# Moving the gMLP's first half ahead of the state-space part, through HBM, with a second buffer for the CT loop

## The chip, the cores and the metric

One Trainium2 chip, one of its cores. The metric is the time of one execution on the device in microseconds (us); lower is better. Each kernel was run several times, beside runs of the kernel before on the same chip. Engines are named as in the profile: PE is TensorE, PEld its weight loads, DVE is VectorE, ACT is ScalarE, POOL is GpSimd, SP is SyncE. A name such as SPq or ACTq is the queue in which that engine issues transfers. PSUM is the memory, in banks, into which PE writes its sums; in this kernel ACT and DVE copy them out (such as Hst<-ps_mm). The granted clock is the share of PE's full clock that the profile shows for a stretch. A line of a timeline reads: start and length in us, engine, line of the kernel, operation, output<-input, shapes, count, and in brackets how long the engine had idled before and what ended that.

## The reference, cut to what matters

The output is the input plus two branches of its layer norm: a state-space convolution (A) and a gated MLP that mixes along the sequence (B). S is 2048, D is 512, N is 128, half of the MLP's width is 688.

```python
x = A_u
xn = _layernorm(x, axis=-1)
return x + _A_ref(xn, A_A_re, ..., A_Dskip) + _B_ref(xn, B_w_in, B_w_sp, B_b_sp, B_w_out)

# A: y = conv(xn, K) + xn * Dskip, where K[d, l] = Re sum_n C * exp(dt * A * l) * dt * B
# B:
z = _gelu(jnp.einsum('bsd,df->bsf', x, w_in))
z1 = z[..., :Fh].copy()
z2 = _layernorm(z[..., Fh:], axis=-1)
g = jnp.einsum('ts,bsf->btf', w_sp, z2) + b_sp[None, :, None]
return jnp.einsum('bsf,fd->bsd', z1 * g, w_out)
```

## The kernel before

The kernel turns A into blocks of 128 steps. The exponential is interpolated at 8 nodes (table E), its transpose ET is regrouped by many small copies into CT, matmuls with CT give the block states Hst, a recurrence over the blocks follows on VectorE, and matmuls of Hst with CWb give G. Inside a block, kappa and Lk do the convolution. B is the GELU part, called z (halves z1 and z2), then the mix over the sequence (the "spatial" groups), then the output product. The order of emission is: layer norm, E, CT loop, w_in and z2, recurrence, G, z1, final loop over eight chunks of 256 rows.

The parts that matter:

```python
# CT loop: 8 turns, ONE buffer, 32 row copies a turn
engs = [nc.scalar, nc.gpsimd]
for dq in range(NDQ):
    CT = sp.tile([P, DQ, 2, N], dt.bfloat16, name="CT", tag="CT")
    for g in range(ND):
        for k in range(KB):
            row = 32 * g + k
            engs[(g * KB + k) % len(engs)].dma_start(
                CT[row:row + 1, :, :, :].rearrange("o d c n -> o (d c n)"),
                ET2[dq * DQ:(dq + 1) * DQ, g, :, k, :])
    ...   # 128 matmuls into 4 PSUM banks, then 4 copies on ACT and 4 on DVE into Hst

# gelu: ACT copy, ACT square, DVE product, ACT sigmoid, DVE product
# z2, row by row: after two gelus
nc.scalar.activation(out=rstd[:], in_=mv[:, 1:2], func=ACT.Sqrt, bias=epsT[:])

# G: four times 256 matmuls and 4 copies (here one round's copies), with the order (dl s) turned into (s dl)
for h in range(4):
    d0 = b * P + h * 32
    nc.any.tensor_copy(out=G[:, :, d0:d0 + 32].rearrange("k s dl -> k dl s"),
                       in_=psg[32 * h:32 * h + KB, :].rearrange("k (dl s) -> k dl s", dl=32))
```

Of the kernel before, what the change touches and what calls it, by code (L numbers as in the profile page):

```python
# [11 lines left out]
dt = mybir.dt  # L12
ACT = mybir.ActivationFunctionType
ALU = mybir.AluOpType
# [3 lines left out]
P = 128  # L18
KB = 8
# [16 lines left out]
def kernel(  # L36
# [18 lines left out]
    nc = tc.nc  # L55
# [4 lines left out]
    S, D = x_flat.shape  # L60
    N = A_A_re.shape[1]
# [49 lines left out]
    G = keep.tile([KB, NT, D], dt.bfloat16, name="G")  # L111
    kapB = keep.tile([P, KB, D], dt.bfloat16, name="kapB")
    Lk = keep.tile([P, KB, P], dt.bfloat16, name="Lk")
# [47 lines left out]
    with tc.tile_pool(name="prep", bufs=1) as pp:  # L161
# [5 lines left out]
        for i, (nm, ap) in enumerate((("are", A_A_re), ("aim", A_A_im), ("bre", A_B_re),  # L167
                                      ("bim", A_B_im), ("cre", A_C_re), ("cim", A_C_im))):
            t = pp.tile([P, D], dt.bfloat16, name="prm_" + nm)
            (nc.sync if i % 2 == 0 else nc.scalar).dma_start_transpose(t[:], ap)  # L170
            prm[nm] = t
# [68 lines left out]
    engs = [nc.scalar, nc.gpsimd]  # L240
    for dq in range(NDQ):
        CT = sp.tile([P, DQ, 2, N], dt.bfloat16, name="CT", tag="CT")
# [44 lines left out]
    onesM = sp.tile([P, P], dt.bfloat16, name="onesM")  # L287
    nc.vector.memset(onesM[:], 1.0)
    cw_flat = CWb[:, 0, :, :].rearrange("p k d -> p (k d)")
    kap_flat = kapB[:].rearrange("p k d -> p (k d)")  # L290
    for i in range(KB * D // TCH):
        psk = psum.tile([P, TCH], dt.float32, name="ps_mm", tag="ps_mm", bufs=PSB)
        nc.tensor.matmul(psk[:], lhsT=onesM[:], rhs=cw_flat[:, i * TCH:(i + 1) * TCH],
                         start=True, stop=True)
        nc.any.tensor_copy(out=kap_flat[:, i * TCH:(i + 1) * TCH], in_=psk[:])

    u_i = sp.tile([P, P], dt.int32, name="u_i")
    nc.gpsimd.iota(u_i[:], pattern=[[1, P]], base=-64, channel_multiplier=-1)
    s_f = sp.tile([P, P], dt.float32, name="s_f")
    nc.vector.tensor_copy(out=s_f[:], in_=u_i[:])  # L300
    nc.vector.tensor_scalar(out=s_f[:], in0=s_f[:], scalar1=1.0 / 64.0, scalar2=None,
                            op0=ALU.mult)
    lk_f = sp.tile([P, P], dt.float32, name="lk_f")
    for k in range(KB):
        c = coefs[k]
        nc.vector.memset(lk_f[:], float(c[0]))
        for sidx in range(1, KB):
            nc.vector.tensor_tensor(out=lk_f[:], in0=lk_f[:], in1=s_f[:], op=ALU.mult)  # L308
            nc.vector.tensor_scalar(out=lk_f[:], in0=lk_f[:], scalar1=float(c[sidx]),
                                    scalar2=None, op0=ALU.add)  # L310
        nc.gpsimd.affine_select(out=lk_f[:], in_=lk_f[:], pattern=[[1, P]],
                                compare_op=ALU.is_ge, fill=0.0, base=0,
                                channel_multiplier=-1)
        nc.scalar.copy(out=Lk[:, k, :], in_=lk_f[:])

# [3 lines left out]
    if dbg in ("ssm", "intra", "inter"):  # L319
        gp = ctx.enter_context(tc.tile_pool(name="gmlp_dbg", bufs=1))  # L320
        for q in range(1, NT - 1):
# [54 lines left out]
    gmlp = ctx.enter_context(ExitStack())  # L376
    gpk = gmlp.enter_context(tc.tile_pool(name="gmlpk", bufs=1))
# [4 lines left out]
    z1T = gpk.tile([P, NF, S], dt.bfloat16, name="z1T")  # L382
    z2n = gpk.tile([P, NT, Fh], dt.bfloat16, name="z2n")
    gpz = ExitStack()
    gp = gpz.enter_context(tc.tile_pool(name="gmlpz", bufs=1))
    xnT = gp.tile([P, ND, S], dt.bfloat16, name="xnT")
    for dtl in range(ND):
        for g4 in range(NT // 4):
            pst = psum.tile([P, TCH], dt.bfloat16, name="ps_tr", tag="ps_tr")
            for i in range(4):  # L390
                q = g4 * 4 + i
                nc.tensor.transpose(out=pst[:, i * P:(i + 1) * P],
                                    in_=xnTok[:, q, dtl * P:(dtl + 1) * P],
                                    identity=ident[:])
            nc.any.tensor_copy(out=xnT[:, dtl, g4 * TCH:(g4 + 1) * TCH], in_=pst[:])
    w_in_sb = gp.tile([P, ND, F], dt.bfloat16, name="w_in_sb")
    nc.sync.dma_start(w_in_sb[:], B_w_in.rearrange("(t p) f -> p t f", p=P))

    SQC3 = math.sqrt(0.044715)
    C1 = 2.0 * math.sqrt(2.0 / math.pi)  # L400

    def gelu(ps_ap, dst_ap, rows, cols):
        zb = gp.tile([P, TCH], dt.bfloat16, name="g_zb", tag="g_zb", bufs=2)
        qd = gp.tile([P, TCH], dt.bfloat16, name="g_qd", tag="g_qd", bufs=2)
        sv = gp.tile([P, TCH], dt.bfloat16, name="g_sv", tag="g_sv", bufs=2)
        nc.scalar.activation(out=zb[0:rows, 0:cols], in_=ps_ap, func=ACT.Copy)  # L406
        nc.scalar.activation(out=qd[0:rows, 0:cols], in_=ps_ap, func=ACT.Square, scale=SQC3)  # L407
        nc.vector.scalar_tensor_tensor(out=sv[0:rows, 0:cols], in0=qd[0:rows, 0:cols],  # L408
                                       scalar=1.0, in1=zb[0:rows, 0:cols],
                                       op0=ALU.add, op1=ALU.mult)  # L410
        nc.scalar.activation(out=sv[0:rows, 0:cols], in_=sv[0:rows, 0:cols],  # L411
                             func=ACT.Sigmoid, scale=C1)
        nc.vector.tensor_tensor(out=dst_ap, in0=sv[0:rows, 0:cols], in1=zb[0:rows, 0:cols],  # L413
                                op=ALU.mult)

    f2_chunks = []
    c0 = 0
    while c0 < Fh:
        c1 = min(Fh, c0 + TCH)
        f2_chunks.append((c0, c1))  # L420
        c0 = c1
    for q in range(NT):
        z2g = gp.tile([P, Fh], dt.bfloat16, name="z2g", tag="z2g", bufs=2)
        for (c0, c1) in f2_chunks:
            ps = psum.tile([P, TCH], dt.float32, name="ps_mm", tag="ps_mm", bufs=PSB)
            for dtl in range(ND):
                nc.tensor.matmul(ps[:, 0:c1 - c0],  # L427
                                 lhsT=xnT[:, dtl, q * P:(q + 1) * P],
                                 rhs=w_in_sb[:, dtl, Fh + c0:Fh + c1],
                                 start=(dtl == 0), stop=(dtl == ND - 1))  # L430
            gelu(ps[:, 0:c1 - c0], z2g[:, c0:c1], P, c1 - c0)
        nsub = 2
        sub = Fh // nsub
        assert Fh % nsub == 0 and sub <= nc.vector.BN_STATS_FMAX
        stats = gp.tile([P, nsub, nc.vector.BN_STATS_DIM], dt.float32, name="z2_stats", bufs=3)
        for si in range(nsub):
            nc.vector.bn_stats(out=stats[:, si, :], in_=z2g[:, si * sub:(si + 1) * sub])  # L437
        mv = gp.tile([P, nc.vector.BN_AGGR_DIM], dt.float32, name="z2_aggr", bufs=3)
        nc.vector.bn_aggr(out=mv[:], in_=stats[:])
        rstd = gp.tile([P, 1], dt.float32, name="z2_rstd", bufs=3)  # L440
        nc.scalar.activation(out=rstd[:], in_=mv[:, 1:2], func=ACT.Sqrt, bias=epsT[:])
        nc.vector.reciprocal(out=rstd[:], in_=rstd[:])
        nc.vector.tensor_scalar(out=z2n[:, q, :], in0=z2g[:], scalar1=mv[:, 0:1],
                                scalar2=rstd[:, 0:1], op0=ALU.subtract, op1=ALU.mult)

# [30 lines left out]
    for ft in range(NF):  # L476
        fs = fsizes[ft]
        for tchk in range(NTC):
            ps = psum.tile([P, TCH], dt.float32, name="ps_mm", tag="ps_mm", bufs=PSB)
            for dtl in range(ND):  # L480
                nc.tensor.matmul(ps[0:fs, :],  # L481
                                 lhsT=w_in_sb[:, dtl, ft * P:ft * P + fs],
                                 rhs=xnT[:, dtl, tchk * TCH:(tchk + 1) * TCH],
                                 start=(dtl == 0), stop=(dtl == ND - 1))
            gelu(ps[0:fs, :], z1T[0:fs, ft, tchk * TCH:(tchk + 1) * TCH], fs, TCH)
    gpz.close()

    gt = gmlp.enter_context(tc.tile_pool(name="gt", bufs=1))
# [7 lines left out]
    for tchk in range(NTG):  # L496
# [3 lines left out]
        tsl = slice(tchk * TCG, (tchk + 1) * TCG)  # L500
        for ft in range(NF):
            fs = fsizes[ft]
            ps2 = psum.tile([P, TCH], dt.float32, name="ps_mm", tag="ps_mm", bufs=PSB)
            for st in range(NT):
                nc.tensor.matmul(ps2[0:fs, 0:TCG], lhsT=z2n[:, st, ft * P:ft * P + fs],  # L505
                                 rhs=wsT[:, st, :], start=(st == 0), stop=False)
# [71 lines left out]
```

## Time and profile before

The median is 600.23 us of the first 5 runs and 600.92 us of the 16 runs beside which the changed kernel was timed; the profiled run spans 598.5 us. The table gives the stages, read off the trace as first start and last end of the named instructions. These six moments are the ruler.

| us from the span's start | before |
|---|---|
| z on ACT | 266.8 to 426.5 |
| first CT copy issued | 121.2 |
| last Hst copy ended (CT loop done) | 255.5 |
| recurrence on DVE | 258.5 to 327.6 |
| G copies | 346.5 to 388.0 |
| first spatial matmul, then end of span | 435.9, 598.5 |

Busy time over the whole span is PE 49%, DVE 64%, ACT 41%, POOL 18%: no engine is full, so the stages must be read one by one. From the first spatial group on, PE is full and nothing else matters; before that, the question is always which engine the next stage waits for.

### The profile page before, as it was taken

The page shows a single profiled execution, that of the slowest core. Times are in us where ns is not written, and L with a number is a line of the kernel's source. Part 1 is how long each engine was busy: PE and PEld are TensorE (multiplying, and loading weights), DVE is VectorE, ACT ScalarE, POOL GpSimd, SP SyncE. Part 2 cuts the span into 40 slices and gives each one's busy share as a digit, 9 for nine tenths or more (in the row PEclk, how much of TensorE's full clock was granted, in tenths as well). Part 3 has the DMA queues.
Part 4 walks back from the last instruction along what each step waited for, and adds up shares of the span by engine and source line. Part 5 has one row for each costly group of instructions (what it writes and reads, how often), then busy time and mean ns, then how long its engine had stood idle before and what let it go on. Part 6 is the DMA issues. An engine that isn't in the chain of part 4 may idle for free.

```text
span 598.5 us, 9154 instructions
## 1 busy us (share of the span) xinstructions
PE 291.5 (49%) x3467; PEld 181.9 (30%) x3480; DVE 381.3 (64%) x942; ACT 246.4 (41%) x360; POOL 106.7 (18%) x176
## 2 busy tenths in 40 slices
PE   0004000250232322483443434365089999999997
PEld 0001000140232222351211332022065566556653
DVE  1999977899664433389999587466715542554253
ACT  1205667611244433368989985899400000000000
POOL 0000000050555654400000000000413113320310
PEclk9999555555555555567555557599589999999999
DMA  7100000000010100040000000000454331433000
GB/s 188 23 0 1 0 1 1 0 19 0 19 20 19 20 19 18 19 142 1 0 1 1 2 4 3 0 1 1 73 121 106 88 78 47 107 90 87 18 19 18
DMA packets 54844, 20.53 MB, mean 34 GB/s; under 512 B 45153, under 2 KB 54289, under 8 KB 54802
## 3 DMA queue, kind: packets, MB, share of 16 engines
q1 hardware_dynamic: 23330, 10.46, 7.1%
q10 hardware_dynamic: 27376, 8.45, 6.1%
q0 software_dynamic: 4096, 1.06, 0.9%
q8 instruction: 27, 0.44, 0.3%
q14 instruction: 15, 0.12, 0.1%
HBM read 6.57 MB, written 2.10 MB: 14 GB/s over the span
## 4 chain that ended last, share of the span: by engine, by line
DVE 31%; PE 29%; ACT 15%; ACTq 12%; issue 6%; DMA 4%; POOL 1%; SPq 0%; DVEq 0%; POOLq 0%
PE ps_mm L505 15%; ACTq L246 11%; PE ps_mm L523 5%; PE ps_mm L534 4%; DVE G L472 4%; ACT Hst L268 3%; DVE g_sv L408 3%; ACT G L472 3%; ACT g_zb L406 2%; DVE z_stats L437 2%; PE ps_mm L507 2%; DVE lk_f L308 2%; DMA prm_cim<-in_A_C_im_dram 2%; ACT g_qd L407 1%; DMA wsT<-in_B_w_sp_dram 1%
## 5 line engine op out<-in xcount | busy, mean ns | idle before, releaser
L505 PE MATMUL ps_mm<-wsT,z2n 128*128 128x256 bf16 (+1 forms) x768 | 93.9, 276 | 19.6 <-DMA wsT<-in_B_w_sp_dram 19.6
L505 PEld LDWEIGHTS <-z2n 128*128 128x128 bf16 (+1 forms) x768 | 72.6, 99 | 34.3 <-issue 21.9
L258 PE MATMUL ps_mm<-m,CT 8*128 8x16 bf16 x1024 | 35.6, 187 | 91.1 <-DMA CT<-ET 83.5
L270 DVE CAST Hst<-ps_mm 128x256 bf16<-128x256 f32 x32 | 40.7, 1377 | 56.0 <-ACT Hst L268 56.0
L268 ACT ACTIVATE Hst<-ps_mm 128x256 bf16<-128x256 f32 x32 | 40.9, 1581 | 77.7 <-DMA CT<-ET 76.7
L246 POOL DMA_DIRECT2D CT<-ET x128 | 64.0, 559 | 48.9 <-PE ps_mm L258 37.2
L509 DVE TENSOR_TENSOR z1T<-ps_mm,z1T 128x256 bf16<-128x256 f32 (+1 forms) x48 | 20.3, 423 | 82.1 <-PE ps_mm L507 82.1
L544 POOL TENSOR_TENSOR cq<-xnTok,dskipB 128x512 bf16<-128x512 bf16 x16 | 19.8, 1242 | 291.4 <-DVE z1T L413 181.0
L258 PEld LDWEIGHTS <-CT 8*128 8x128 bf16 x1024 | 33.0, 103 | 93.8 <-issue 85.0
L427 PE MATMUL ps_mm<-w_in_sb,xnT 128*128 128x176 bf16 (+1 forms) x125 | 33.2, 429 | 39.5 <-ACT g_qd L407 39.1
L519 DVE TENSOR_TENSOR xk<-xnTok,kapB 128x1024 bf16<-128x1024 bf16 x64 | 42.1, 729 | 1.0
L231 PE MATMUL ps_tr<-ident,E 128*128 128x128 bf16 x64 | 9.0, 302 | 61.1 <-DVE E L217 59.3
L481 PE MATMUL ps_mm<-xnT,w_in_sb 128*128 128x512 bf16 (+1 forms) x94 | 27.6, 432 | 22.9 <-ACT g_qd L407 14.7
L408 DVE SCALAR_TENSOR_TENSOR g_sv<-g_qd,g_zb 128x512 bf16<-128x512 bf16 (+2 forms) x56 | 31.5, 586 | 9.2 <-ACT g_qd L407 9.2
L427 PEld LDWEIGHTS <-xnT 128*128 128x128 bf16 x128 | 16.0, 129 | 55.5 <-issue 53.3
L406 ACT ACTIVATE g_zb<-ps_mm 128x512 bf16<-128x512 f32 (+2 forms) x56 | 29.2, 521 | 6.4 <-DVE z2g L413 6.3
L411 ACT ACTIVATE g_sv<-g_sv 128x512 bf16<-128x512 bf16 (+2 forms) x56 | 29.2, 548 | 4.9 <-DVE g_sv L408 4.7
L523 PE MATMUL ps_mm<-xk,Lk 128*128 128x512 bf16 x120 | 29.9, 379 | 0.4
L223 PE MATMUL ps_mm<-xnTok,PhiU 128*128 128x512 bf16 x16 | 6.5, 579 | 48.1 <-DVE py_b L153 48.1
L407 ACT ACTIVATE g_qd<-ps_mm 128x512 bf16<-128x512 f32 (+2 forms) x56 | 29.2, 521 | 0.0
L472 DVE CAST G<-ps_mm 8x512 bf16<-8x512 f32 x9 | 22.1, 2456 | 8.3 <-ACT G L472 8.1
L231 PEld LDWEIGHTS <-E 128*128 128x128 bf16 x64 | 6.4, 136 | 63.8 <-DVE E L217 60.6
(120 smaller groups left out, 544.4 us busy)
## 6 DMA issues: line engine op xcount, KB each, us to landing
xTok<-in_A_u_dram SPq DMA_DIRECT2D x1, 2048.0 KB, 12.1
CT<-ET ACTq DMA_DIRECT2D x128, 8.0 KB, 1.9
CT<-ET POOLq DMA_DIRECT2D x128, 8.0 KB, 1.8
xq<-in_A_u_dram ACTq DMA_DIRECT2D x16, 128.0 KB, 2.2
out_dram<-res SPq DMA_DIRECT2D x16, 128.0 KB, 1.7
w_in_sb<-in_B_w_in_dram SPq DMA_DIRECT2D x1, 1376.0 KB
w_out_sb<-in_B_w_out_dram ACTq DMA_DIRECT2D x5, 128.0 KB, 6.1
dskipB<-in_A_Dskip_dram SPq DMA_DIRECT2D x1, 128.0 KB
```

Source lines behind the costliest of these rows:

```text
L246: engs[(g * KB + k) % len(engs)].dma_start(CT[row:row + 1, :, :, :].rearrange("o d c n -> o (d c n)"), ET2[dq * DQ:(dq + 1) * DQ, g, :, k, :])
L258: nc.tensor.matmul(banks[g][:, c * 256 + dl * NT: c * 256 + (dl + 1) * NT], lhsT=CT[32 * g:32 * g + KB, dd, c, :], rhs=m4[32 * g:32 * g + ...
L268: nc.scalar.activation(out=dst_ap, in_=src_ap, func=ACT.Copy)
L270: nc.vector.tensor_copy(out=dst_ap, in_=src_ap)
L406: nc.scalar.activation(out=zb[0:rows, 0:cols], in_=ps_ap, func=ACT.Copy)
L407: nc.scalar.activation(out=qd[0:rows, 0:cols], in_=ps_ap, func=ACT.Square, scale=SQC3)
L408: nc.vector.scalar_tensor_tensor(out=sv[0:rows, 0:cols], in0=qd[0:rows, 0:cols], scalar=1.0, in1=zb[0:rows, 0:cols], op0=ALU.add, op1=ALU. ...
L427: nc.tensor.matmul(ps[:, 0:c1 - c0], lhsT=xnT[:, dtl, q * P:(q + 1) * P], rhs=w_in_sb[:, dtl, Fh + c0:Fh + c1], start=(dtl == 0), stop=(dt ...
L472: nc.any.tensor_copy(out=G[:, :, d0:d0 + 32].rearrange("k s dl -> k dl s"), in_=psg[32 * h:32 * h + KB, :].rearrange("k (dl s) -> k dl s", ...
L505: nc.tensor.matmul(ps2[0:fs, 0:TCG], lhsT=z2n[:, st, ft * P:ft * P + fs], rhs=wsT[:, st, :], start=(st == 0), stop=False)
L519: nc.vector.tensor_tensor(out=xk4[:], in0=xnTok[:, qs[0]:qs[0] + QPC, :], in1=kapB[:, k:k + 1, :].to_broadcast((P, QPC, D)), op=ALU.mult)
L523: nc.tensor.matmul(psfs[i][:, 0:D], lhsT=Lk[:, k, :], rhs=xk4[:, i, :], start=firsts[i], stop=False)
```

## The change

Its intent is to have ACT's long GELU work lie beside the build of E and off the path behind the CT loop, to let the loads of one CT turn run beside the matmuls of another, to spare most table loads for square roots, and to have G, kappa and Lk share the space that is then free. z1 and z2 go to HBM and come back. The core of the diff:

```diff
+    z2n_d = dram.tile([S, Fh], dt.bfloat16, name="z2n_d")
+    z1T_d = dram.tile([NF, P, S], dt.bfloat16, name="z1T_d")
+    ...   # xnT, w_in, gelu, z2 and z1 now stand here, ahead of the SSM, in a pool of their own
+        if q % RB == RB - 1:        # RB = 4: one Sqrt for four rows
+            nc.scalar.activation(out=rstd[:], in_=mv[:, :, 1], func=ACT.Sqrt, bias=epsT[:])
+            ...
+                nc.sync.dma_start(z2n_d[qq * P:(qq + 1) * P, :], z2s[:])
...
-    engs = [nc.scalar, nc.gpsimd]
+    engs = [nc.sync, nc.gpsimd]
...
-        CT = sp.tile([P, DQ, 2, N], dt.bfloat16, name="CT", tag="CT")
+        CT = sp.tile([P, DQ, 2, N], dt.bfloat16, name="CT", tag="CT", bufs=2)
...
-    ...   # kappa and Lk from here (ahead of z), z1 from behind G
+    nc.sync.dma_start(z2n[:], z2n_d.rearrange("(q p) f -> p q f", p=P))
     for q in range(1, NT - 1):      # recurrence, then G
+    ...   # kappa and Lk here, behind G
...
+            z1c = gt.tile([P, TCG], dt.bfloat16, name="z1c", tag="z1c", bufs=3)
+            nc.gpsimd.dma_start(z1c[0:fs, :], z1T_d[ft, 0:fs, tsl])
```

## The prediction

> **What bounds the kernel now.** I read the page's slices first, then the chain of work that ended last, then the timeline inside the stages that the chain names. The slices (each is 1/40 of the span, 15 us):
>
> ```profile
> PE   0004000250232322483443434365089999999997
> DVE  1999977899664433389999587466715542554253
> ACT  1205667611244433368989985899400000000000
> POOL 0000000050555654400000000000413113320310
> PEclk9999555555555555567555557599589999999999
> ```
>
> No engine bounds the whole; stages follow one another. From the windows and the chain I cut it so: 0 to 33 us loads and the layer norm; 33 to 48 the interpolation polynomials (DVE alone); 48 to 121 the tables E; 121 to 255 the CT stage (column 9 to 17: nothing above 6 tenths except a filling DVE at its start); 255 to 427 the gMLP first half with its GELUs, here called z (ACT at 8 or 9 tenths); 427 to 598 the final loop, PE full at clock 0.99. So 134 us of CT hold almost idle PE and ACT, and 172 us of z need ACT and DVE. One turn of CT, from the timeline:
>
> ```profile
> 190.77 5.02 ACT L268 ACTIVATE Hst<-ps_mm 128x256 bf16<-128x256 f32 x4 [8.78 <-DMA CT<-ET]
> ...
> 193.81 7.95 POOL L246 DMA_DIRECT2D CT<-ET  x16 [6.00 <-PE ps_mm L258]
> 194.16 10.22 ACTq L246 DMA_DIRECT2D CT<-ET  x16
> 198.34 1.06 PEld L258 LDWEIGHTS <-CT 8*128 8x128 bf16 x32 [4.93 <-issue]
> ```
>
> The 32 small loads of a turn wait until PE has let go of the only CT buffer (POOL idle 6.00), then take 8 us to issue on POOL and 10.2 us on ACT. The last lands 1.9 us later, PE does 1.1 us, and the turn closes: the ACT copies begin at 163.05, 176.76, 190.77, 204.43 us, so 13.8 us a turn, eight turns. It is a bound by issue, not by bytes: 20 GB/s. Why z does not fill the hole shows in the queue waits:
>
> ```profile
> SPq L397 <- DMA CT<-ET: 233.9, 2, 230.3
> ```
>
> The load of w_in for z waits 230 us for CT: z's tiles lie where the SSM tiles lay. In z, a row costs (ACT timeline):
>
> ```profile
> 282.89 0.60 ACT L406 ACTIVATE g_zb<-ps_mm 128x512 bf16<-128x512 f32 x1 [0.47 <-DVE z2g L413]
> ...
> 284.41 1.28 ACT L441 ACT_TABLE_LOAD   x1
> 285.71 0.29 ACT L441 ACTIVATE z_rstd<-z_aggr,epsT 128x1 f32<-128x1 f32 x1
> 286.02 1.28 ACT L411 ACT_TABLE_LOAD   x1
> 287.31 0.87 ACT L411 ACTIVATE g_sv<-g_sv 128x512 bf16<-128x512 bf16 x2
> 288.66 0.60 ACT L406 ACTIVATE g_zb<-ps_mm 128x512 bf16<-128x512 f32 x1 [0.47 <-DVE z2g L413]
> ```
>
> 5.77 us from one g_zb to the next, 2.57 of it two table loads for one square root. Under z the recurrence and the G copies run; the G copies go one at a time (chain):
>
> ```profile
> 371.72 2.44 ACT G L472
> 374.18 2.43 ACT G L472
> ```
>
> ACT and DVE never copy G at once, although they take turns: 16 copies of 2.45 us are 39 us (346 to 388). In the final loop PE is the path: a chunk takes 19.65 us (435.89 to 594.7, eight chunks), of which 12.4 us are the six spatial groups of L505 and the rest L523 and L534.
>
> **What the Trainium skill says.** "ScalarE: Activation LUTs", What ACT_TABLE_LOAD costs: 1283 ns for the load plus about 1380 ns of drain, for each switch of set. The trace agrees on 1283 (33 loads in z, mean 1283) but the square root starts 1.30 us after the load began (284.41 to 285.71), so no such drain is seen; I count 1.28. "DMA: Bandwidth & Descriptors", Issuing engines are not separate DMA queues: all issuers share the same 16 engines, another issuer saves only sequencer time. Here that sequencer time is the bound (10.2 us of issue against 20 GB/s), so moving half of the issues to SP frees ACT but is no bandwidth. "DMA: Bandwidth & Descriptors", Anatomy of one DMA: about 2 us fixed; CT's median is 1.9 us to landing. "TensorE: Matmul & The Clock Gate", Part 1: a PE that idles falls to half its clock. The trace agrees: granted clock 0.50 in CT, 0.99 in the final loop.
>
> **The change part by part.** (1) z moves ahead of the whole SSM, with tiles of its own; z1 and z2 go through HBM. (2) The square roots of four rows are batched. (3) CT gets two buffers, SP issues instead of ACT. (4) G, kappa and Lk move after CT, and z2n is loaded back. The order of emission is taken as priority, with later work filling holes, as DVE's Lk does today.
>
> z: starts at 37 us (33, and 4 for the first transposes). A row without tables is 5.77 - 2.57 = 3.2 us; 16 are 51. Four batches at 2 x 1.28 + 0.3 = 2.9 make 12. The row stores with two buffers wait for a landing about once per batch: 4 x 2 = 8, an estimate. The z1 half was 39 us (388 to 427). z ends at 37 + 51 + 12 + 8 + 39 = 147. In its shadow lie the polynomials (15 us of DVE) and m4.
>
> E: 73 us today with the Lk fill; the loop itself is 8 turns of 6.4 us (chain: 75.74, 88.89, 102.04 are two turns apart) = 52. ACT is the busy engine of z, so little of E fits under it; what does fit swaps tables. I take 50 us more, with the last transposes: 197.
>
> CT: with two buffers a turn is the longer issue. SP should be as ACT, 16 x 0.608 = 9.7 us; POOL's 8.1 and the copies' 5.0 lie beside it. 8 x 9.7 + 7 for the last landing, PE and copies = 85 against 134: ends at 282. The products for CWb (48 x 0.68 = 33 us DVE) fit beside.
>
> After CT nothing of z is left to hide behind. Recurrence: 112 DVE operations, 0.335 us apart when back to back (261.67, 262.00, 262.34): 37.5 us, to 320. The G matmuls' start 3, G copies 39: 362. Lk (56 pairs, 0.58 us apart, 33 us), which was free fill in E and CT, and kappa now share DVE with the G copies: 8 us exposed. Final psums may start at 370.
>
> Final loop: 157 us of PE. z2n is 2.8 MB; at the input load's 2 MB in 12.1 us that is 17 us, then two wsT at 6 to 8 us, all beside the recurrence. So the spatial groups of two chunks, 2 x 12.4 = 25 us, can run before 370; hgc and wsT have two buffers and allow no more. Left: 157 - 25 = 132, plus 4 for a PE gone cold (first group 3.57 against 1.85 us) and a tail of 4. 370 + 140 = 510. The z1c loads (6 a chunk on POOL at 0.55) lie beside 19.65 us of PE, with POOL's own 4.8.
>
> Sum of changes: CT stage -49, tables in z -29 (16 x 2.57 less 12), idle hidden or moved the rest, against the recurrence, G and Lk that come out of z's shadow.
>
> **The rivals.** (a) Table thrash: if E's 24 activations slip singly between z's sigmoids, each costs two loads, up to 48 x 1.28 = 61 us less the 16 loads there now. For it: ACT has a hole of 0.3 to 0.5 us a row and a filler knows no tables. Half of it: about 540. (b) CT stays at 13.8 a turn because SP's issue is slower than ACT's or a wait orders the loads behind the copies: +33, about 543. Against it: the wait named is the one buffer. (c) The tail after CT is fully serial, z2n and wsT late because their space frees last, and PE prepares nothing: +25 to +40, about 545. (d) Better: DVE, half idle in z, takes most of E and Lk slips under CT: -35, about 475.
>
> **Range and chances.** 510 is the middle; (d) sets the low end, one of (a) to (c) the high: 478 to 550. All of (a) to (c) together make some 600, so a slower kernel needs all at once. Faster by over 2% 0.93, within 2% 0.04, slower 0.03.
>
> **What would show it.** Table loads under L441's successor: about 4; total about 33 or fewer, where (a) shows over 45. CT turns about 9.7 us apart with the issuing SP never waiting long for PE; (b) shows 13. First L505 before the G copies end, and PE idle between the second chunk and the end of G. G copies still one at a time, 39 us. z over near 147 and CT begun near 195. If CT begins before 150 or the final loop has holes at each chunk, my order of stages is wrong.

## The result, and the profile after

The changed kernel takes 566.54 us in the median of 9 runs (565.1 to 569.0), the kernel before 600.92; the ratio is 0.9431 with a 95% interval of 0.9416 to 0.9446. "Faster by over 2%" was right; 566.5 lies 16.5 us above the range.

The slices of the page of the kernel after (each 14.2 us):

```profile
PE   0146533354454665333333001341799999999997
DVE  0999976866655699974445999475587454355343
ACT  1347799999999995444544000278600000000000
POOL 0000000000000007977750799000124433542420
PEclk9999555555655565555555555555699999999999
```

z and E now fill ACT from column 5 to 14, and the CT loop (15 to 21) still leaves ACT at 4 or 5 tenths and PE mostly at 3. The new thing is column 22 to 27: a valley of nearly 90 us, in which first DVE alone works (22 to 24) and then ACT and DVE by halves, before PE fills. In the kernel before, the same engines were busy with z there.

What E does in z's stretch, from ACT's timeline:

```profile
100.22 1.28 ACT L140 ACT_TABLE_LOAD   x1
101.51 0.87 ACT L140 ACTIVATE g_sv<-g_sv 128x512 bf16<-128x512 bf16 x2
102.40 1.28 ACT L297 ACT_TABLE_LOAD   x1
103.69 0.63 ACT L297 ACTIVATE emag<-argr 128x512 f32<-128x512 f32 x1
104.34 1.28 ACT L176 ACT_TABLE_LOAD   x1
105.64 0.30 ACT L176 ACTIVATE z_rstd<-z_aggr,epsT 128x4 f32<-128x4 f32 x1
105.84 0.58 ACT L135 ACTIVATE g_zb<-ps_mm 128x512 bf16<-128x512 f32 x1
...
113.29 0.58 ACT L135 ACTIVATE g_zb<-ps_mm 128x512 bf16<-128x512 f32 x1
```

Most of E's 24 exponentials and sines (0.63 us each) stand alone between sigmoids: 21 of them need a load of 1.28 us, and the sigmoids need 19, where without E among them they need 6 (a5 below). A row of z, g_zb to g_zb, takes 7.45 us here. The kernel makes 49 table loads, the one before made 53.

The queue in which w_in waited 230 us no longer has such a wait; the row stores wait for z instead, and they keep nobody (waits of SP's queue: what waited, for what, total us, times, longest):

```profile
SPq L184 <- DVE z2s L181: 98.2, 8, 28.0
```

A turn of the CT loop, timeline of the kernel after:

```profile
243.50 18.70 SPq L332 DMA_DIRECT2D CT<-ET  x27
...
246.49 1.43 ACT L354 ACTIVATE Hst<-ps_mm 128x256 bf16<-128x256 f32 x1 [1.12 <-PE ps_mm L344]
...
252.08 7.94 POOL L332 DMA_DIRECT2D CT<-ET  x16 [3.03 <-PE ps_mm L344]
```

SP now issues without a break: 27 copies in 18.70 us, 0.69 us each. POOL waits 3.03 us for the matmuls and then does its 16 in 7.94 us. From the first issue (213.6) to the last Hst copy (310.8) the loop takes 97.2 us, where it took 134.3.

The G copies in the chain of work:

```profile
369.70 2.44 ACT G L506
372.17 2.43 ACT G L506
```

They are as before, one at a time, 16 of them. But now nothing runs beside them that PE could use. The tail, from the timelines of that stretch:

```profile
313.02 4.02 DVE L483 TENSOR_TENSOR rec_t<-ar,Hst 128x512 bf16<-128x512 bf16 x1
313.36 3.39 POOL L598 TENSOR_TENSOR cq<-xnTok,dskipB 128x512 bf16<-128x512 bf16 x3
...
320.20 32.53 POOL L599 TENSOR_TENSOR cq<-cq,xq 128x512 bf16<-128x512 bf16 x1 [3.46 <-DMA xq<-in_A_u_dram]
...
356.06 5.88 ACTq L550 DMA_TRANSPOSE wsT<-in_B_w_sp_dram  x1
...
361.99 0.61 ACT L518 CAST kapB<-ps_mm 128x512 bf16<-128x512 f32 x1 [52.47 <-issue]
...
399.92 3.57 PE L560 MATMUL ps_mm<-wsT,z2n 128*128 128x256 bf16 x16 [4.60 <-ACT kapB L518]
```

A DVE operation of 0.41 us takes 4.02 us while POOL runs its three cq products, and then one POOL operation is held for 32.53 us while DVE runs the recurrence. xq's next loads sit in ACT's queue behind the cq buffers that this POOL operation keeps; the transposed load follows them; so ACT touches nothing from about 310 to 361.99. The first spatial group comes at 399.92, after the banks of kappa are emptied. z2n had landed at 321.6.

### The profile page after: what moved, and what is told of

Its sections match the earlier page's. It is cut to its first block, busy times and chain, and to the rows that moved or that the text cites. A ratio compares the mean times of both kernels' runs of the same rounds, so it can differ in the third digit from the quotient of the medians.

```text
span 566.8 us, 9301 instructions
## 1 busy us (share of the span) xinstructions
PE 308.4 (54%) x3466; PEld 185.4 (33%) x3480; DVE 373.0 (66%) x922; ACT 254.2 (45%) x352; POOL 161.5 (28%) x224
## 4 chain that ended last, share of the span: by engine, by line
PE 28%; ACT 23%; DVE 22%; issue 9%; DMA 8%; SPq 5%; POOL 3%; ACTq 2%; DVEq 0%; POOLq 0%
PE ps_mm L560 13%; SPq L332 5%; PE ps_mm L577 4%; ACT G L506 4%; PE ps_mm L588 4%; ACT g_zb L135 3%; ACT g_qd L136 3%; DMA CT<-ET 3%; ACT L140 2%; ACT g_sv L140 2%; DMA z2n<-z2n_d 2%; POOL CT L332 2%; DMA prm_cim<-in_A_C_im_dram 2%; DVE bn_stats L94 2%; PE ps_mm L562 2%
## 5 line engine op out<-in xcount | busy, mean ns | idle before, releaser
L354 ACT ACTIVATE Hst<-ps_mm 128x256 bf16<-128x256 f32 x32 | 42.6, 1331 | 48.8 <-PE ps_mm L344 48.6
L190 PE MATMUL ps_mm<-xnT,w_in_sb 128*128 128x512 bf16 (+1 forms) x94 | 41.1, 610 | 39.3 <-ACT g_qd L136 39.0
L564 DVE TENSOR_TENSOR hgc<-ps_mm,z1c 128x256 bf16<-128x256 f32 (+1 forms) x48 | 20.2, 422 | 62.8 <-PE ps_mm L562 62.8
L344 PEld LDWEIGHTS <-CT 8*128 8x128 bf16 x1024 | 33.0, 103 | 57.8 <-issue 30.6
L599 POOL TENSOR_TENSOR cq<-cq,xq 128x512 bf16<-128x512 bf16 x16 | 50.3, 3147 | 4.5 <-DMA xq<-in_A_u_dram 3.5
L160 PE MATMUL ps_mm<-w_in_sb,xnT 128*128 128x176 bf16 (+1 forms) x125 | 31.3, 413 | 35.6 <-ACT g_qd L136 35.3
L557 POOL DMA_DIRECT2D z1c<-z1T_d x48 | 26.4, 550 | 67.0 <-DVE hgc L564 36.5
L501 PE MATMUL ps_mm<-Hst,CWb 128*8 128x16 bf16 x1024 | 10.5, 196 | 61.7 <-DVE Hst L486 42.8
L190 PEld LDWEIGHTS <-w_in_sb 128*128 128x128 bf16 (+1 forms) x96 | 13.5, 141 | 65.1 <-issue 64.4
L506 ACT CAST G<-ps_mm 8x512 bf16<-8x512 f32 x13 | 31.6, 2428 | 6.8 <-DVE G L506 6.6
L501 PEld LDWEIGHTS <-CWb 128*8 128x8 bf16 x1024 | 9.6, 99 | 63.4 <-DVE Hst L486 42.9
```

What stands on the lines that cost most here:

```text
L160: nc.tensor.matmul(ps[:, 0:c1 - c0], lhsT=xnT[:, dtl, q * P:(q + 1) * P], rhs=w_in_sb[:, dtl, Fh + c0:Fh + c1], start=(dtl == 0), stop=(dt ...
L190: nc.tensor.matmul(ps[0:fs, :], lhsT=w_in_sb[:, dtl, ft * P:ft * P + fs], rhs=xnT[:, dtl, tchk * TCH:(tchk + 1) * TCH], start=(dtl == 0), ...
L344: nc.tensor.matmul(banks[g][:, c * 256 + dl * NT: c * 256 + (dl + 1) * NT], lhsT=CT[32 * g:32 * g + KB, dd, c, :], rhs=m4[32 * g:32 * g + ...
L354: nc.scalar.activation(out=dst_ap, in_=src_ap, func=ACT.Copy)
L599: nc.gpsimd.tensor_tensor(out=cq[:], in0=cq[:], in1=xq[:], op=ALU.add)
```

## The experiments

Where one moment on the ruler is compared, it is read from the trace of that run. "After" is the changed kernel; differences in us are of medians. The edits are shortened: `...` and comments stand for code left out.

| kernel | median us | ratio to before (95%) | CT issued | CT loop done | first spatial |
|---|---|---|---|---|---|
| before | 600.9 | 1 | 121.2 | 255.5 | 435.9 |
| after | 566.5 | 0.9431 (0.9416 to 0.9446) | 213.6 | 310.8 | 399.9 |
| b1_sqrt4 | 598.2 | 0.9966 (0.9942 to 0.9989) | 121.3 | 255.9 | 434.7 |
| b2_ct2 | 571.6 | 0.9533 (0.9505 to 0.9561) | 121.9 | 219.7 | 406.5 |
| b3_sqrt4_ct2 | 568.0 | 0.9458 (0.9440 to 0.9476) | 121.8 | 219.7 | 403.4 |
| a1_ct1buf | 586.8 | 0.9773 (0.9752 to 0.9793) | 213.8 | 329.5 | 418.8 |
| a3_act_free | 559.3 | 0.9306 (0.9283 to 0.9328) | 213.5 | 309.8 | 391.9 |
| a4_early | 576.3 | 0.9599 (0.9573 to 0.9625) | 212.3 | 310.4 | 377.4 |
| a5_e_after_z | 566.3 | 0.9418 (0.9388 to 0.9449) | 212.5 | 309.9 | 398.1 |
| s2_ssm_first_gate | 573.9 | 0.9554 (0.9535 to 0.9573) | 117.0 | 214.3 | 405.4 |
| c0_issue3 | 551.8 | 0.9193 (0.9173 to 0.9213) | 212.3 | 295.9 | 383.4 |
| c1_z1_in_ct | 541.0 | 0.9011 (0.8988 to 0.9034) | 167.9 | 274.3 | 371.1 |
| c2_gflat | 561.8 | 0.9355 (0.9326 to 0.9384) | 212.8 | 309.0 | 382.1 |
| c3_spatial | 560.1 | 0.9332 (0.9304 to 0.9360) | 213.6 | 308.2 | 323.6 |
| e1_gpsum | 548.6 | 0.9127 (0.9104 to 0.9149) | 212.1 | 308.2 | 381.3 |
| e2_lk | 559.8 | 0.9320 (0.9296 to 0.9345) | 216.0 | 311.1 | 394.4 |
| e3_sp_g_lk | 535.4 | 0.8917 (0.8885 to 0.8949) | 215.6 | 311.0 | 327.0 |
| e4_all | 506.8 | 0.8441 (0.8413 to 0.8469) | 170.5 | 277.0 | 302.2 |

All gave correct results.

### Which part of the change carries the gain

**b1_sqrt4**: the kernel before with the square roots of four rows batched.

```diff
-    mv = ...(1 row); rstd = Sqrt(mv) per row
+    mv = ...(RB = 4 rows); one Sqrt of 128x4 per four rows
```

> The kernel before with the square roots of four rows batched and nothing else. If the table loads are the path of z: 24 of 33 loads go, 24 x 1.28 = 31 us, so about 570. Rival, VectorE is the path there (it was busy 74 of the 84 us from 262 to 346, because the recurrence is mixed in): only the 10 us that it idled can go, about 590.

29 table loads in place of 53, and 2 us. The loads had not been on the path, as the rival said. z runs there with the recurrence mixed in, and DVE is the full engine: in b1's own trace it is busy 74.8 of the 75 us from 268 to 343, ACT 49.4.

**b2_ct2**: the kernel before with two CT buffers and SP in ACT's place as issuer.

```diff
-    engs = [nc.scalar, nc.gpsimd]
+    engs = [nc.sync, nc.gpsimd]
-        CT = sp.tile([P, DQ, 2, N], dt.bfloat16, name="CT", tag="CT")
+        CT = sp.tile([P, DQ, 2, N], dt.bfloat16, name="CT", tag="CT", bufs=2)
```

> The kernel before with two CT buffers and SP in place of ACT as issuer, nothing else. If the CT stage is on the path: turns fall from 13.8 to the 11.4 us of the changed kernel, 8 turns, so -20 us, about 580. Rival, CT's end is hidden behind VectorE's fill: less than 5 us.

The CT loop falls from 134.3 to 97.8 us, the time by 29 us, more than I had expected. The loop before was not just eight turns of 13.8 us, which make 110: between the last issue of its first turn (133.9) and ACT's first of the second (151.8) lies a gap of 18 us, in which POOL waited 18.8 us for DVE's steps of Lk and ACT 13.7 us for POOL's. In b2 the second turn follows at once (134.5 to 134.6). These two lines give 29 of the change's 34 us; in this order no run takes the buffer and the issuer apart.

**b3_sqrt4_ct2**: both of them, nothing moved.

```diff
+    RB = 4                                # b1's edit
+    engs = [nc.sync, nc.gpsimd]           # b2's edit
+        CT = sp.tile(..., bufs=2)
```

> Both small parts on the kernel before, z and SSM left in their order. If the two gains are in stages that follow one another they add: between 570 (b1 at -10) and 550 (b1 at -30). At 550 the two small parts alone beat the whole change (566.5) and moving z in front of the SSM would be worth less than nothing; at 570 the move is worth about nothing.

568.0 us: within 0.3% of the whole change, without any trip through HBM. The ruler shows why the move is worth nothing. From b3 to the changed kernel, CT starts 91.8 us later (121.8 to 213.6), the loop is as long (97.9 and 97.2), and from its end to the first spatial group 183.7 us become 89.1, which is 94.6 less; the final stretch costs 3.7 us more (163.2 and 166.9). So +91.8 - 0.7 - 94.6 + 3.7 is 0.2 us. z was carried from one place where it was the path to another where it is the path; the recurrence and G, which z had covered, came into the open.

**a1_ct1buf**: the changed kernel with the second CT buffer taken away again.

```diff
-        CT = sp.tile([P, DQ, 2, N], dt.bfloat16, name="CT", tag="CT", bufs=2)
+        CT = sp.tile([P, DQ, 2, N], dt.bfloat16, name="CT", tag="CT")
```

> The changed kernel with one CT buffer again, SP still issuing. Theory, the second buffer lets issue run on while PE and the landing of the turn before finish: turns go back from 11.4 to about 14, +20 us, about 587. Rival, a turn is SP's 16 issues at 0.635 us whatever the buffers: below +5.

The loop grows from 97.2 to 115.7 us and the time by 20: in the new order that is what the second buffer is worth. With one buffer the turns from the second to the last begin 14.1 us apart, in the kernel before 14.4, so the other issuer by itself hardly shortened a turn. The loop is shorter than the 134.3 us of the kernel before because the gap behind the first turn is gone (first to second turn 14.8 us in place of 30.6); Lk's steps no longer stand there.

### What E under z is worth

**a5_e_after_z**: E's node table is made to depend on the last full tile of z1 (a product with zero, added), so that E cannot run under z.

```diff
+        nc.vector.tensor_scalar(out=g0[:], in0=z1_last[:, 0:1], scalar1=0.0, ...)
-            nc.vector.memset(tk_row[:, k, :], float(tk_nodes[k]))
+            nc.vector.tensor_scalar(out=tk_row[:, k, :], in0=g0[:], scalar1=1.0,
+                                    scalar2=float(tk_nodes[k]), op0=ALU.mult, op1=ALU.add)
```

> The changed kernel with E held back by data (its node table is computed from z's last full tile), so no E activation can fall between z's sigmoids. Table loads from about 49 in all to about 30, 19 x 1.28 = 24 us less ACT work, but E's 50 us are no longer under z. Theory, mixing saved no more than its tables cost: CT begins within 10 us of today's 213.6 and the time within 10 us of 566. Rival, hiding E under z is where the change gains: 25 to 50 us slower.

The same time, and CT begins at 212.5 in place of 213.6. Its windows (busy us of each engine in the stretch, then the clock, DMA share and GB/s):

```profile
44.00:156.00 112.00, 60.86 (x234) 25.49 (x236) 90.00 (x264) 97.91 (x195) 0.00 (x0) 0.79 0.15 50
156.00:213.00 57.00, 6.27 (x44) 4.46 (x45) 36.60 (x63) 40.56 (x50) 0.00 (x0) 0.50 0.01 2
```

The fourth busy figure is ACT's. Alone, z lasts from 44.2 to 155.7 with ACT at 98 of 112 us, and E with its transposes 57 us more. Under z, E cost just as much: 18 more table loads (49 against 31) are 23 us by themselves.

**s2_ssm_first_gate**: z is emitted behind the CT loop, and its first two GELUs wait for E.

```diff
-    ...   # z2, z1 ahead of the SSM
+    ...   # z2, z1 behind the CT loop
+    nc.scalar.activation(out=zgate[:], in_=E[:, 1, 0, D - 1:D], func=ACT.Copy, scale=0.0, bias=1.0)
-        nc.scalar.activation(out=zb[...], in_=ps_ap, func=ACT.Copy)
+        nc.scalar.activation(out=zb[...], in_=ps_ap, func=ACT.Copy, scale=zgate[:, 0:1])  # first two
```

> The changed kernel with z emitted after the CT loop (own tiles kept), and its first GELUs held back by data until E is done, so that z falls beside CT and not in front of E. Theory, the order was the wrong one: CT begins near 125 as before, ends near 220, z ends near 260 beside it and the recurrence: 480 to 510. Rival, z beside CT delays CT's evictions on ACT and VectorE so much that nothing is won: above 545.

CT now starts at 117.0, and yet the time is 7 us worse. I had expected z to lie beside the CT loop. PE's timeline shows it did not:

```profile
210.51 1.12 PE L296 MATMUL ps_mm<-m,CT 8*128 8x16 bf16 x32 [1.62 <-DMA CT<-ET]
...
211.57 0.61 PE L327 MATMUL ps_mm<-w_in_sb,xnT 128*128 128x512 bf16 x1
```

The first matmul of z stands in PE's queue behind the last of CT. What was only emitted later ran later here, however idle PE was.

**c1_z1_in_ct**: so z1's 24 tiles go into the loop's body, three behind each turn's matmuls.

```diff
+        for (ft, tchk) in z1_tiles[3 * dq:3 * dq + 3]:
+            z1_tile(ft, tchk)     # 4 matmuls, gelu; stored to HBM one turn later
+    ...   # and each turn's CT loads are emitted one turn earlier, ahead of those stores
```

> The changed kernel with the 24 tiles of z1 taken out of the stretch before the node table and put into the CT loop, three after each turn's matmuls (their stores one turn later). Theory, hiding E under z cannot pay since both live on ScalarE, whereas the CT loop leaves ScalarE idle for 50 of its 97 us: a z1 tile holds ScalarE for about 1.6 us, so three make 4.8 us beside 5.3 us of Hst copies in a turn of 11.5 us, and they fit. CT then starts 24 x 1.6 = 38 us earlier less what the table loads keep, and the loop grows by 0 to 12 us: 20 to 35 us less than the changed kernel (531 to 547, ratio 0.885 to 0.91). Rival, PE or the banks of PSUM bind (PE at half clock takes 12 matmuls of about 0.6 us more in each turn, some 7 us beside 4.5 to 5): the turn grows by 4 us or more and the gain is under 10 us.

CT starts 45.7 us earlier (167.9), the loop is 9.2 us longer (106.4), and 18.8 us go to the last z1 tiles and their stores before the recurrence starts at 293.1; for 11.8 of them ACT stands still, behind a transposed load in its queue. So the recurrence starts 17.4 us earlier: the first place found where part of z really is covered. The rest of the 25.5 us comes later: POOL's cq products are done before the recurrence, which then takes 37.7 us in place of 42.5, and the first G copy follows it by 5.9 us in place of 9.5.

### What sets the CT turn

**c0_issue3**: of 32 copies a turn SP issues 12, POOL 15 and ACT 5.

```diff
-    engs = [nc.sync, nc.gpsimd]
+    pat = [nc.sync, nc.gpsimd, nc.sync, nc.gpsimd, nc.scalar, nc.gpsimd, nc.sync, nc.gpsimd]
+    engs = pat * 3 + [nc.sync, nc.gpsimd, nc.sync, nc.gpsimd, nc.scalar, nc.gpsimd, nc.sync, nc.scalar]
```

> The changed kernel with one thing altered: of the 32 row copies of each turn SyncE issues 12, GpSimd 15 and ScalarE 5, in place of 16 and 16. Theory, SyncE's issues set the turn of the CT loop: in the changed kernel they follow one another at 0.635 us, so 16 take 10.2 us of a turn of some 11.5; 12 take 7.6 us, GpSimd's 15 take 7.4 us, and ScalarE has 3.2 us of issues on top of 5.3 us of its Hst copies. The turn falls to about 9 us and the time by 15 to 22 us against the changed kernel (544 to 552, ratio to the kernel before 0.905 to 0.92). Rival, the turn is set by the wait of the transfers for a free CT buffer and by the landing (about 2 us) plus PE's 128 matmuls: then the turn stays above 11 us and the time is within 5 us of the changed kernel's 566.

The loop falls from 97.2 to 83.6 us and the time by 14.7, just under what the theory said. Only the issuers changed, so issue does hold the turn. The mean, (83.6 - 7) / 8 = 9.6 us by my own allowance of 7 us for the ends, hides that the turns do fall to the 9 us expected: from the fourth on PE begins them 8.9 us apart (249.5, 258.9, 267.2, 276.1, 285.1). What is left over is one hole ahead of them:

```profile
239.43 1.09 PE L346 MATMUL ps_mm<-m,CT 8*128 8x16 bf16 x32 [7.77 <-DVE Hst L358]
```

PE waits for a PSUM bank, and DVE makes its first Hst copy only at 238.1, 17.8 us after ACT's first; until then it works on the products for CWb almost without a break.

### What holds the tail

**a3_act_free**: xq's loads and all transposed loads are issued by SP.

```diff
-                nc.scalar.dma_start(xq[:], x_flat[q * P:(q + 1) * P, :])
+                nc.sync.dma_start(xq[:], x_flat[q * P:(q + 1) * P, :])
-        (nc.sync if tchk % 2 == 0 else nc.scalar).dma_start_transpose(
+        nc.sync.dma_start_transpose(
```

> The changed kernel with all tail loads (xq, every wsT) issued from SP, none from ACT. Theory: after the recurrence ACT's queue stood until 361.99 us behind an xq load that waited for POOL's cq and behind a 5.9 us transpose issue, so the G copies began 9 us after the recurrence ended (353.0 to 362.5); freed, they begin at about 354 and the time falls by 7 to 9, to 558. Rival, the G copies wait for PE or psum: under 2 us.

7.2 us less; the G copies start at 356.7 in place of 362.5 and the first spatial group comes 8 us earlier. Loads that waited in ACT's queue had held its copies back. The two kinds of load were moved together, so their shares are not shown.

**a4_early**: kappa and Lk are emitted ahead of the recurrence.

```diff
+    ...   # kappa and Lk, ahead of sctx.close(), tables in the pool that stays
     sctx.close()
     ...   # recurrence, G
-    ...   # kappa and Lk
```

> The changed kernel with kappa and Lk computed before the SSM tiles are given up, as the kernel before did (their temporaries in a pool of their own, one buffer shared in the preparation to make room). Theory: PE's first spatial group ran at 399.9 only because the eight kappa matmuls stood ahead of it in PE's queue, waiting for psum whose eviction stood behind G copies and Lk on ACT and VectorE; without them PE prepares up to two chunks during the G copies: 15 to 25 us, 542 to 552. Rival, PE could not start early for its data (z2n, wsT) or the G copies are all that counts: under 5 us.

10 us slower, so that theory fell. With kappa out of the way the first spatial group did come 22.5 us earlier, at 377.4 and ahead of the first G copy (383.9), but right behind the first matmuls of G, which stand in PE's queue before it and waited 62.1 us for the recurrence. And the recurrence had grown. DVE's timeline:

```profile
317.66 0.35 DVE L519 TENSOR_TENSOR Hst<-Hst,rec_t 128x512 bf16<-128x512 bf16 x1
317.94 0.27 DVE L398 TENSOR_TENSOR lk_f<-lk_f,s_f 128x128 f32<-128x128 f32 x1
318.13 0.41 DVE L524 TENSOR_TENSOR rec_t<-ai,Hst 128x512 bf16<-128x512 bf16 x1
```

Lk's steps sit between those of the recurrence on the engine that the recurrence fills, and it lasts from 316.1 to 379.2, 63 us in place of 42. In the changed kernel the same work ran beside the G copies. Moving it ahead put it on the path.

**c2_gflat**: G is laid out as (k, d, s), so that a copy writes one unbroken run.

```diff
-    G = gpk.tile([KB, NT, D], dt.bfloat16, name="G")
+    G = gpk.tile([KB, D, NT], dt.bfloat16, name="G")
-            nc.any.tensor_copy(out=G[:, :, d0:d0 + 32].rearrange("k s dl -> k dl s"), ...)
+            nc.any.tensor_copy(out=G[:, d0:d0 + 32, :].rearrange("k dl s -> k (dl s)"), ...)
-   ... rhs=G[:, q - 1, :]
+   ... rhs=G[:, :, q - 1]
```

> The changed kernel with G laid out as (k, d, s) in place of (k, s, d), so that each of its 16 copies writes one unbroken run of 512 elements and no two touch the same stretch; the 15 later matmuls read G with a stride. Theory, the 16 copies of 2.43 us follow one another whichever engine has them and lie on the path from the recurrence to the final phase: they fall to 0.5 to 0.6 us each, so 16 x 1.85 = 30 us of them go, of which the kappa and Lk work beside them (about 10 us each) keeps 5 to 10: 18 to 28 us less than the changed kernel (538 to 548, ratio 0.895 to 0.912). Rival, the final phase starts late for another cause (the transposed load on ScalarE's queue, the chain of Lk): then the time falls by under 10 us.

The first spatial group comes 17.8 us earlier, and the time falls by only 4.8. The groups of tile G in this run (duration min, median, max in ns) show one of the reasons:

```profile
L582 PE MATMUL ps_mm<-G,PhiY x15: 1070/1072/1092, 410.9 to 552.0; 8*128 8x512 bf16 x15
L506 ACT CAST G<-ps_mm x13: 569/577/586, 360.2 to 383.3; 8x512 bf16<-8x512 f32 x13
```

A copy went from 2.43 to 0.58 us, but the 15 later matmuls, which now read G with a stride, went from 0.384 to 1.07 us, and they stand where PE is full: 15 x 0.69 is 10.3 us.

**e1_gpsum**: G keeps its layout, and the matmuls write PSUM in the order (s, dl) instead.

```diff
-        nc.tensor.matmul(psg[32 * h:32 * h + KB, dl * NT:(dl + 1) * NT],
+        nc.tensor.matmul(psg[32 * h:32 * h + KB, :].rearrange("k (s dl) -> k dl s", dl=32)[:, dl, :],
-            out=G[:, :, d0:d0 + 32].rearrange("k s dl -> k dl s"), in_=psg[...].rearrange("k (dl s) -> k dl s", dl=32)
+            out=G[:, :, d0:d0 + 32], in_=psg[...].rearrange("k (s dl) -> k s dl", dl=32)
```

> The changed kernel with G's layout kept, but its matmuls writing PSUM in the order (s, dl), so that a copy reads PSUM straight and writes runs of 32 elements. Theory, the flat G lost its gain to its 15 later matmuls (1.07 us in place of 0.38 us, 10.3 us of a TensorE that is 95% busy there): with copies of 0.6 to 0.7 us and the later matmuls at 0.38 the first spatial group comes at about 382 and the time falls by 12 to 17 us (549 to 554, ratio 0.914 to 0.923). Rival, the gain is lost to the granted clock or the Lk chain: 561 again.

```profile
L582 PE MATMUL ps_mm<-G,PhiY x15: 374/384/385, 410.1 to 538.4; 8*128 8x512 bf16 x15
L506 ACT CAST G<-ps_mm x13: 570/577/582, 359.4 to 382.5; 8x512 bf16<-8x512 f32 x13
```

Both are fast in this run, and the time falls by 17.9 us, just over the theory's range. The stride of G cost c2 13.2 us, of which the 10.3 are seen; the other 3 may be the clock, 0.95 in its last 131 us where the kernel after has 1.00, and stay open.

**c3_spatial**: the twelve spatial groups of the first two chunks are emitted between the steps of the recurrence.

```diff
+        if q >= 3 and early:            # in the loop of the recurrence
+            spatial(*early.pop(0))
```

> The changed kernel with the twelve spatial groups of the first two chunks put into the program between the recurrence's steps, ahead of the matmuls of G on TensorE. My prediction had these groups prefetched for nothing; in the changed kernel TensorE's queue has G's matmuls and kappa's ahead of them, and it idles through the recurrence. Theory, order in TensorE's queue is what kept them back: 25 us of the final phase move into the recurrence, the recurrence grows by 12 x 0.42 = 5 us plus waits for the first group (z2n lands 11 us after the recurrence starts, the transposed load some 5 us later): 8 to 18 us less than the changed kernel (548 to 558, ratio 0.912 to 0.93). Rival, VectorE, which has to multiply each group out between the steps, waits for TensorE and the recurrence grows by as much as is saved: within 5 us of 566.

```profile
310.00:353.00 43.00, 24.60 (x169) 17.58 (x169) 41.03 (x104) 0.00 (x0) 25.83 (x18) 0.72 0.65 166
...
372.00:405.00 33.00, 12.30 (x558) 6.60 (x558) 27.41 (x60) 24.10 (x17) 1.81 (x3) 0.50 0.01 3
405.00:425.00 20.00, 10.36 (x51) 5.60 (x51) 15.73 (x52) 0.89 (x3) 0.88 (x3) 0.72 0.00 0
```

These are its windows, PE first. The groups were kept back by PE's queue, as the theory had it: they now run from 323.6 on, and PE is busy 24.6 of 43 us in which it had 1.3. Only 6.4 us of it reach the end. The recurrence grows to 50.6 us (from 42.5), and from 372 to 425 PE stands idle for 30 of 53 us, because what is left of these chunks needs G, kappa and Lk (PE waits 9.4 us for Lk alone). In the changed kernel the second chunk's spatial groups filled such waits (418 to 436); moved away, they leave them empty.

**e2_lk**: Lk, which depends on no input, is computed by POOL at the start of the kernel.

```diff
+    Lk = keep.tile([P, KB, P], dt.bfloat16, name="Lk")    # ahead of the layer norm
+            nc.gpsimd.tensor_tensor(out=lk_f[:], in0=lk_f[:], in1=s_f[:], op=ALU.mult)
+            nc.gpsimd.tensor_scalar(out=lk_f[:], in0=lk_f[:], scalar1=float(c[sidx]), ...)
-            nc.vector.tensor_tensor(...); nc.vector.tensor_scalar(...)   # behind kappa
```

> The changed kernel with the Lk tables, which depend on no input, computed by GpSimd at the start, where it idles for 200 us, in place of VectorE and ScalarE beside G's copies. Theory, alone this frees nothing, since G's copies of 2.43 us one at a time and kappa's banks still hold TensorE to about 395: 0 to 6 us less than the changed kernel. Rival, Lk is the chain that holds G's copies apart: 10 us or more less. It may cost a few us if GpSimd's operations hold up VectorE's with two inputs in the first 100 us.

6.7 us less, just over the theory's range: worth a little alone, and not the chain that held the rest.

**e3_sp_g_lk**: c3, e1 and e2 together.

```diff
+            spatial(*early.pop(0))                                   # c3's edit
+    psg[...].rearrange("k (s dl) -> k dl s", dl=32)[:, dl, :]         # e1's edit
+    Lk = keep.tile(...)                                              # e2's edit
```

> The three changes of the tail together: first twelve spatial groups ahead of G's matmuls in the queue, G's matmuls writing PSUM in (s, dl) order, Lk at the start on GpSimd. Theory, each masked the other: with all, 25 us of TensorE's work lie in the recurrence, G's stage falls from 47 to about 30 us, and what is left of the final phase, some 132 us, follows at once: 25 to 40 us less than the changed kernel (526 to 541). Rival, they do not add up (TensorE's clock or VectorE binds): less than 15 us.

535.4 us, 31.1 less than after. The total I expected was right, the reason was not: alone they gave 6.4, 17.9 and 6.7, which make 31.0. They do not mask one another; they add. The longer recurrence that limits c3 is here too (49.8 us), and behind it PE still idles for 20 of the 34 us from 361 to 395, while G is made.

**e4_all**: e3, c1 and a3 together.

```diff
+    ...   # e3's three edits
+            z1_tile(ft, tchk)                                        # c1's edit
+                nc.sync.dma_start(xq[:], ...)                        # a3's edit
```

> The same three, and z1 inside the CT loop, and xq's and the transposed loads issued by SyncE. If the gains add, 25 for z1 and 25 to 40 for the tail with some 3 to 7 for ScalarE's queue: 495 to 515, which is the time I had predicted for the change itself (ratio 0.825 to 0.86). If z1's stay in the CT loop ends in a tail that then waits for the loads, 515 to 530.

506.8 us, 15.6% under the kernel before and 10.5% under the changed one. It beats both. Its slices (each 12.6 us):

```profile
PE   0128654324200655878775009943689999999996
ACT  1346759999977644899986300003500000000000
```

The CT loop (13 to 21) now has PE and ACT at 4 to 9 tenths, and PE works in the recurrence (24, 25). Of the 63.8 us of the three gains (c1 25.5, e3 31.1, a3 7.2), 59.8 arrive. By the profiled runs the loss lies behind the recurrence: from its end to the end of the span e3 saves 41.7 us, c1 6.0 and a3 7.6, together 55.3, and e4 saves 44.1; up to there e4 does 2.7 us better than the sum. Both c1 and a3 shorten the same gap between the recurrence and the first G copy (9.5 us after, 5.9 and 4.7 in these, 5.0 in e4), which explains some 4 us; the rest is not taken apart.

## Why the prediction was wrong

It came to 510.0 and the profiled run spans 566.8. Along its own moments:

| step of the prediction | predicted | after | adds to the miss |
|---|---|---|---|
| CT starts | 197 | 213.6 | +16.6 |
| CT loop | 85 | 97.2 | +12.2 |
| recurrence, to its last operation | 37.5 | 42.2 | +4.7 |
| from there to the final phase | 50 | 46.9 | -3.1 |
| the final phase | 140 | 166.9 | +26.9 |

These make 57.3; the prediction had rounded up half a microsecond.

- **z and E.** z alone was sized well: 110 us foretold, 111.5 measured in a5, in part by luck, since none of the 8 us allowed for waits on the row stores shows there. It starts at 44, not 37: the layer norm ends at 33.6 as foretold, but the first transposes and their copies take until 43.7, 10 us in place of 4. "I take 50 us more" for E was 7 us short (a small part of it in the sum: a turn of E, put at 6.4 us, is 6.6 by the chain's own times): the stretch from z's end to CT is 57 us, and hiding part of E under z saves none of it (a5). Rival (a), table thrash, was real, with 49 loads where the prediction had named over 45 as its sign, but it is no extra cost: what E hides, the loads eat.
- **CT.** The mechanism was right: the second buffer gains, and issue sets the turn (a1, c0). The pitch was mis-sized: "16 x 0.608 = 9.7 us" took the median busy time of an issue for the distance between two, although the prediction's own line has ACT's 16 issues at 10.22 us. SP's 128 issues take 91.8 us from the first to the end of the last, 11.5 us a turn. Rival (b) did not come. That the old loop's 134 us were more than eight turns of 13.8, by the gap behind the first (b2), was not seen.
- **Recurrence.** 37.5 us of DVE work is what it is, plus some 4 us in which one operation stands while POOL runs its cq products. In c1, where these are done before, the recurrence takes 37.7 us.
- **G, kappa, Lk.** The stretch was sized right by luck: the copies were one at a time as said, ACT's first copy of G came 9.5 us after the recurrence, half of it because of loads in its queue (4.7 us in a3), which was not foreseen, and the first spatial group came before the last G copy.
- **Final phase.** The step that failed most is "the spatial groups of two chunks, 2 x 12.4 = 25 us, can run before 370". None did. For the first chunk the data was there (z2n at 321.6, the transposed weights wsT at 326.5), but PE's queue has the matmuls of G and kappa first, and the first group ran at 399.9. The second chunk's wsT came only at 364.1, since its load stood in ACT's queue. Rival (c) described the outcome with another cause (data that comes late), and I gave it too little weight. c3 shows that order in the queue was the cause, the groups then run from 323.6, and that even so only 6 of the 25 us arrive.
- **The sum.** "CT stage -49, tables in z -29" gave the credit wrongly. In the order before, the CT part alone is worth 29 us (b2) and the tables alone 2 (b1). "Idle hidden or moved the rest" is nothing: b3 has no move and is within 0.3% of the change. What z had been covering at the back was priced right, 87.5 us from CT's end to the final phase against 89.1 measured; the saving hoped for at the front, E under z, was not there, and nor were the 25 us of spatial groups.

That 506.8 us come so near to 510 is no merit of the prediction; e4 gets there by z1 in the loop and by shorter copies, neither of which it had.

What stays open: the 3 us of c2, what the buffer and the issuer are worth apart in the order before, and what of c3's 25 us is lost to which wait.

## What to carry to other kernels

Before moving a long stage, ask what it covers where it stands: a stage moved from beside one thing to beside another gains only if the new neighbour leaves its engine idle and the queues interleave the two. Here PE took matmuls in the order of its queue (s2, c3), so work hid only where it was emitted between, not where there was idle time; and loads that waited in ACT's queue kept ACT idle (310 to 362 us). Put the small parts of a change in alone first: here two lines gave 29 of 34 us.

## What the Trainium skill lacked or had wrong

- "DMA: Bandwidth & Descriptors", Issuing engines are not separate DMA queues, calls the issuer's time usually small relative to the transfer. Here it is the bound: 27 issues of 8 KB copies in 18.70 us, 0.69 us each, and giving a few to a third issuer took 14.7 us off the kernel (c0). I found no page that gives this pitch for SP.
- "PSUM — Partial Sum Buffer", Specifications, says that any access to PSUM that is not contiguous slows matmuls significantly. The 1024 matmuls of G write 16 values each 128 bytes apart in e1 and have the same median, 0.198 us, as with contiguous writes in the changed kernel; the first and last start lie 29.2 us apart against 30.2. Such ends are modelled in the profile, but the kernel is 17.9 us faster.
- "ScalarE: Activation LUTs", What ACT_TABLE_LOAD costs: the load is 1.28 us as stated, the drain is not seen after the change either: the load at 104.34 begins 0.02 us after the activation before it has ended (103.69 + 0.63), and the next activation begins at 105.64.
- "SBUF — State Buffer", SBUF: two separate sides, has the exclusive lock between GpSimd and a VectorE operation with two SBUF inputs, and the trace agrees (4.02 us for a DVE operation of 0.41). What it does not say is how long an unbroken stream of VectorE operations can hold one GpSimd operation: 32.53 us here (spans on POOL are rough), for one that otherwise takes 1.2 us.
